# A table fill with 32 and 96 rows outermost instead of 29 and 91

## The chip, the cores and the metric

The kernel runs on one core of one Trainium2 chip. The metric is the device time of one execution in microseconds (us). A core has a tensor engine (TensorE, in the profile PE, its weight loads PEld), VectorE (DVE), ScalarE (ACT), GpSimd (POOL) and SyncE (SP), each with an instruction list of its own, and 16 DMA engines that all queues share. A DMA is issued by one of the engines' sequencers (SPq is SP's) and runs later on the DMA engines.

## The reference

The input x has 8 batches of 1856 tokens with 256 features. The reference takes the real part of a two-dimensional Fourier transform of each batch, and feeds the 14,848 resulting rows to a mixture of experts: 4 groups of 4 experts, one expert chosen for each token.

```python
X = np.fft.fft(x, axis=1)
X = np.fft.fft(X, axis=2)
x = X.real.reshape(B * S, D)                # 14848 rows of 256
g_idx = argmax(x @ w_group)                 # one of 4 groups, with its softmax weight g_w
e_idx = argmax(x[mask_g] @ w_expert[g])     # one of 4 experts of the group, weight e_w
h  = np.maximum(x[mask_e] @ w1[g, e], 0.0)  # 256 -> 1024
ye = h @ w2[g, e]                           # 1024 -> 256
out[tok_idx] = (g_w * e_w)[:, None] * ye
```

## The kernel before

**Two phases.** Phase 1 goes over the batches in rounds 0 to 8. In a round, the next batch is loaded (`load_half`, L424, two halves of 1028 KB into a pool `xq`) and folded on VectorE and ScalarE (`fold`, tiles AC, BD and the halves `ghl`), the current batch is transformed along the tokens on TensorE (`s_stage`, PSUM tile `pu`, result `U`), and the batch before it is transformed along the features (`d_stage`, PSUM tiles `pr` for the rows and `pl` for the logits), its rows are stored to a DRAM table `XT` (`rows`, L682 and L685), and its tokens are routed (`route`). Phase 2 takes the experts one after the other: it splits their weights into half-precision parts (`whl`), gathers the tokens' rows (`xg`), transposes them by DMA (`xT<-xh`, L1043), runs the two layers on TensorE (L1066 and L1082) and scatters the results to `out`.

**The slot table T.** Routing writes an entry (row in XT, token, weight: 12 bytes) for each token at the next free position of its expert. T is a DRAM table with room for ROWS rows of 128 entries (1536 bytes) for each of 16 experts, experts one behind the other. Entries that no token takes must read as "no token", so T is filled beforehand from an SBUF tile `tinit`, in which every partition holds one such row of 128 entries. `init_table` does this in round 0 with DMAs on SP's queue. The access patterns on both sides have the table's row outermost (one row per partition of `tinit`), then the expert (on the source side the same data repeated), then the 384 numbers of a row:

- the first fill (L297, called at L303) covers rows 0 to FIRST of all 16 experts; FIRST is 29, the rows of 128 that the tokens of the first two batches can reach;
- a closing row (L305);
- eight later fills (L297, called through `rest`) cover rows FIRST to ROWS, 29 to 120, of two experts each. They are hung up under the letter `t` of the orders below, four in round 1 and four in round 2.

The scatters of entries (`scatter`, L793, DMAs issued by GpSimd, 14 or 15 per batch) have to come after all fills written before them in the program. Among themselves, and the later fills after scatters of earlier batches, they are declared independent.

**What sets the order.** VectorE, ScalarE and TensorE keep in phase 1 the order in which the steps are written, which the strings START, ORDER0, ORDER, ORDER7 and ORDER8 spell out, a letter a step. The fills on SP keep their order in the program too. Other instructions, other DMAs of SP among them, are placed by the framework's planner, which runs a timeline of its own costs.

**The small copies.** For each batch, ScalarE scales a row for feature 128 (`un<-UN`, two instructions per batch; the tile `un` has one buffer), and SP copies it into row 127 of `U` (L625) and in two pieces into the leftover tile `Um` (L627). The first products of `d_stage` that take the second half of `U` wait for the copy, and the `un` of the next batch waits until the copies have read the tile. In SP's list of round 0 and 1 come, in this order: the last loads of the start, the closing row, two halves of x, the first fill, another half of x, the copy to `U`, the two to `Um`, and then further halves of x, fills and stores of rows.

**From the routing to phase 2.** Two experts have slots that are closed early (waves): SP loads their table rows (`early_t`, L898), which waits for the scatters up to then; GpSimd gathers their tokens. All else of phase 2 waits until the last scatter has landed and SP has read the table (`trow<-T`, L919).

Of the kernel before, what the change touches and what calls it, by code (L numbers as in the profile page):

```python
# [8 lines left out]
F32 = mybir.dt.float32  # L9
# [5 lines left out]
PSUM = bass.MemoryType.PSUM  # L15
# [5 lines left out]
P = 128  # L21
KO, KE = 464, 465           # odd / even k of 0..928
NK = KO + KE                # 929
NT = 7                      # full tiles of 128 k of a batch
NL = NK - NT * P            # 33 left: 31 k, then k = 0 and 928, which have no -k
NC = 2 * NT                 # token columns of a batch: k and -k of each tile
NCM = NC + 1                # ... and for each second batch what is left of two batches: 2 * (33 + 31)
PROWS = (2 * NC + 1) * P    # tokens of two batches
FIRST = -(-2 * S // P)       # ... that two batches can reach
ROWS = 120                  # table rows (of 128 entries) of an expert  # L30
CAP = ROWS * P
TROWS = NE * ROWS + 1
NSLOT = 7                   # static slots of an expert
NOVF = 12                   # static overflow slots
UB = 4
XGB = 10
NEARLY = 2                  # experts whose first slots run on the tokens of the first batches,
WAVES = '3:3 5:5'           # in waves: last batch of the tokens, end of the slots
W0_AT = 4                   # round in which the load of the first expert's weights starts
WPART = 1024                # columns of a piece of a split of weights  # L40
LPARTS = 4                  # pieces of their load
LASTZ = 7                   # last round whose routing may go on in the next
EARLY_LAG = 1               # rounds from the tokens of a wave to their gathers
# a step of a split of weights per RATE of products: T1 for a block of layer 1 and slot, T2 for a slot of layer 2
RATE, T1, T2 = 1000, 320, 2570
# Orders of the steps of phase 1, which the arithmetic engines keep: before the rounds, then in rounds 0, 1..6, 7 and 8.
# G, H: batch 0, and d = 128 of all batches, come in; F, N: folds of the next batch and of the one after it, l: their
# lower halves; Y: transforms of d = 128, U: its rows; S: transforms of a batch, and out of PSUM s, I, i: upper halves,
# their subtraction, lower halves; D: features of the last batch, d: their way out, L: its leftovers; R, Z: routing of
# the last batch and of the one before it; t: loads and fills that nothing waits for yet; W, X: weights and tokens of  # L50
# the first job of phase 2
# [6 lines left out]
RS = 2.0 ** -11             # scale of the stored rows  # L58
E23 = 2.0 ** 23             # one, in the exponent of a float32

# powers of two of a batch: scale of x, of the weights' divisors, of the d = 128 rows, of the logits
V_X, V_DIV, V_NY, V_LG, V_LE = range(5)
NV = 5
# columns of the float32 constants
# [13 lines left out]
# columns of the float16 constants  # L78
# [8 lines left out]
def waves():  # L87
    """(last batch, first slot, end of the slots) of each wave."""
    r, a = [], 0
    for w in WAVES.split():  # L90
        b, e = map(int, w.split(":"))
        r.append((b, a, e))
        a = e
    return r
# [7 lines left out]
def _features():  # L102
    """Order of a row's features: [1..127, 0 | 255..129, 128]."""
    return np.concatenate([np.arange(1, 128), [0], 256 - np.arange(1, 128), [128]])
# [12 lines left out]
def _constants():  # L117
# [10 lines left out]
    # rows: A = cos part d = 0..127; B = sin part d = 1..127, then the cos part d = 128  # L128
# [51 lines left out]
def _layout(x, w_group, w_expert, w1, w2):  # L180
    """Only moves data: folds' operands side by side, features in row order."""
    s = np.arange(465)
    idx = np.stack([s, 928 - s, (S - s) % S, 928 + s], 0)      # A, C, B, D
    use = np.ones((4, 465), bool)
    use[2, 0] = False       # s = 0: only x[0] and x[928]
    use[3, 0] = False
    use[1, 464] = False     # s = 464: only x[464] and x[1392]
# [20 lines left out]
def pow2s(V, pool, sumsq, n, tag, outs):  # L208
    """Powers of two around sqrt(sumsq), 2^(e - 63): 2^(m e + a - 127) for each (m, a) of outs; and e."""
# [12 lines left out]
def top(ap):  # L222
    """Upper halves of float32 numbers [128, n]: they, cut to bfloat16."""
    return ap.bitcast(mybir.dt.bfloat16).rearrange("p (n t) -> p n t", t=2)[:, :, 1]


class InOrder:
    """An engine whose instructions keep the order in which they are written."""
# [12 lines left out]
def finish(steps, between=lambda: None):  # L241
    """Runs a generator of steps, and something after each; its result."""
    try:
        while True:
            next(steps)
            between()
    except StopIteration as e:
        return e.value


def bc(ap, axis, n):
    """ap with a repeated axis of n put in at axis."""
    a = ap.unsqueeze(axis)
    shape = list(a.shape)
    shape[axis] = n
    return a.broadcast_to(shape)


class K:
    """The program: pools, constants and the steps of the two phases."""  # L260
# [7 lines left out]
    # ---------------------------------------------------------------- phase 1  # L268
# [16 lines left out]
    def init_table(self, fp):  # L285
        """Entries of no token: first the rows that the first batches can reach, then in parts the others."""
# [22 lines left out]
    def router_in(self):  # L309
        """One scale for the columns of the groups, one for those of the experts: their square sums."""  # L310
# [11 lines left out]
    def router_scale(self, pn):  # L322
        V, sm = self.V, self.sm
        ei, (self.sw,) = pow2s(V, sm, pn, 2, "w", [(-1, 198)])
        # exponents of the logits' factors: that of x, less a bias of 127, and that of the weights
# [5 lines left out]
    def router_weights(self):  # L331
        """R.W in float32 (the logits straight from U), scaled to halves."""
# [27 lines left out]
    def nyquist_in(self):  # L360
        """The column d = 128 of all batches, folded and scaled per batch; the router's scales."""
# [38 lines left out]
    def nyquist(self):  # L400
        """Its cos transforms (rows b)."""
# [28 lines left out]
    def fold(self, b, x, fp, parts=1):  # L430
        """Folds and halves of batch b, in steps; fds[b] is (halves, powers of two)."""
# [5 lines left out]
        def halves(eo, h, i=0):  # L437
            """x[d] +- x[256 - d]; for B and D with the sign that makes all quarters sums"""
# [22 lines left out]
        def squares(h, i, j):  # L461
            """Square sum of a part of x"""
            junk = hl.rearrange("p h m e n -> p (h m e n)").bitcast(mybir.dt.bfloat16)  # halves come later
# [18 lines left out]
        BD = fp.tile([P, 2, 2, 512], F32, name="BD")            # later the results  # L482
# [20 lines left out]
        if b == 0:  # L503
            # the parts that the first products need come first
# [41 lines left out]
        if b > 1:  # L546
            # square sum of all features
# [29 lines left out]
    def later(self, letter, f):  # L577
        """Work that the orders of the steps name by a letter of its own."""
        self.queues[letter].append(f)

    def s_stage(self, b, U):
        """U = cos and sin transforms along s, transposed: U[part][hi/lo] of [128, k]."""
# [4 lines left out]
        for par, tr in parts:  # L587
            k0, n = ((KO, KE), (0, KO))[par]
            # cos: even k from sums, odd from differences; sin the other way round
# [15 lines left out]
    def split_later(self, pu, hi, lo, m):  # L605
        """Halves of a sum in PSUM: what the upper ones leave is found by the tensor engine, in place."""
# [7 lines left out]
    def nyquist_rows(self, b, U, up):  # L614
        """The row of d = 128, in the scale of the batch."""
# [14 lines left out]
    def left(self, b):  # L630
        """Columns in the merged tile, number and sign of what the full tiles leave."""
# [3 lines left out]
    def leftovers(self, b, U):  # L635
        """What is left of k beside that of the other batch of the pair."""
# [8 lines left out]
    def d_stage(self, b, U, pl, rp):  # L645
        """Rows (both signs) to the table of rows; the logits."""
# [4 lines left out]
        for t0 in range(0, len(tiles), 2):  # L651
# [16 lines left out]
            row = rp.tile([P, 2, 2, 256], F32, name="row")         # sign, tile  # L668
# [18 lines left out]
    def route(self, b, pl):  # L687
# [45 lines left out]
        # divisors of the weights: sums of exponentials + 1e-9 (the fifth of each), scaled  # L733
# [9 lines left out]
        # onehot over (g, e), column last  # L743
# [12 lines left out]
        # positions: tokens of the expert up to this column, less those of this column from here on  # L756
# [34 lines left out]
    def scatter(self, group, out, ap, in_, last):  # L791
        """Indirect write of rows; the rows of a group are all different, so none waits for another."""
# [6 lines left out]
    def phase1(self):  # L799
        tc, nc, cp, ps = self.tc, self.nc, self.cp, self.ps  # L800
        with tc.tile_pool(name="xq", bufs=3) as xp, tc.tile_pool(name="fft", bufs=1) as fp, \
# [21 lines left out]
            def run(gens, order, rest=True, keep="N"):  # L823
                """A step of what each letter names; then what the generators have left, but for N."""
# [52 lines left out]
    # ---------------------------------------------------------------- phase 2  # L877
    def slot_info(self, src, n, tag):
        """Columns per slot: row in XT (int), token (int), weight, from table rows [n, 128, 3]."""
# [10 lines left out]
    def early_rows(self, i, b, r0, r1):  # L890
        """Slots r0..r1 of the first experts are closed: later tokens go behind them."""
# [5 lines left out]
        for e in range(NEARLY):  # L897
# [3 lines left out]
            self.tc.add_to_no_dep_group("T", ins.ins)       # no later scatter writes there  # L901
        self.early_t[i] = t

    def early_gather(self, i, b, r0, r1):
        """... and their rows fetched."""
# [18 lines left out]
    def overflow_info(self, qp):  # L924
        """Tiles beyond the static slots: expert and table row of the o-th, o on partitions."""
# [33 lines left out]
        # experts of the overflow tiles, and how many are left to the loop, on partition 0  # L959
# [9 lines left out]
    def load_weights(self, wp, e, pin=False):  # L969
        """e: number or register of the expert."""  # L970
# [11 lines left out]
    def split_steps(self, wp, st, V, A, M, pn, lag=0):  # L982
        """float32 weights of an expert -> halves hi, lo and 1 / scale (powers of two); lag: idle steps
# [288 lines left out]
```

## Time and profile before

| | |
|---|---|
| time, median of 3 runs | 934.24 us (932.9 to 935.9) |
| profiled execution, first to last instruction (its span) | 935.2 us |
| profiled execution's own time beside the span | none is given; the three runs lie around the span |
| PE busy | 817.5 us (87%) |
| DVE busy | 538.9 us (58%) |
| ACT busy | 601.1 us (64%) |
| POOL busy | 398.0 us (43%) |
| DMA | 148.34 MB, 159 GB/s over the span |
| issue of the first fill, of the last later fill | 21.2 us, 93.3 us |
| first and last scatter to T | 98.2 us, 276.8 us |

The busy shares are means over stages with different limits, so the profile is read by stretches. In a row of a timeline, the columns are start and length in us, the engine, the line of the kernel, the operation, what it writes and reads, the count, and in brackets how long the engine had been idle and what ended that. Lines in helpers (L237) stand for every instruction that keeps the written order; there the tiles' names tell the step. For an SP row the length is that of issuing, not of the transfer.

### The profile page before, as it was taken

Reading aid. Unit: us, or ns where it says so; the run is one execution under the profiler, and the core shown is the slowest. Engines: PE = TensorE matmul, PEld = TensorE weight load, DVE = VectorE, ACT = ScalarE, POOL = GpSimd, SP = SyncE. Lnnn points to the kernel's source line nnn. Section 1 sums busy time; section 2 is a strip of 40 time slices with the busy share of each in tenths; the row PEclk is TensorE's granted clock in tenths of the full one; section 3 lists DMA queues with packets and bytes.
Section 4 is the critical chain, followed back from the end, with each engine's and each line's share of the span. In section 5 each row is a group of like instructions: output and inputs, shape, how many; then the busy total and the mean of one; then the engine's idle time right before and its main releaser. Section 6 shows DMA issues by size and latency. Waiting matters only on the chain.

```text
span 935.2 us, 17786 instructions
## 1 busy us (share of the span) xinstructions
PE 817.5 (87%) x6469; PEld 591.9 (63%) x6469; DVE 538.9 (58%) x1207; ACT 601.1 (64%) x1208; POOL 398.0 (43%) x376
## 2 busy tenths in 40 slices
PE   4539889479468969999998999999999999999996
PEld 1226567246247846777867686767778686866775
DVE  7718889336344637465756566465657566573530
ACT  4428768367324758686867778686778777683631
POOL 0000678777775751443333353433333353511112
PEclk9859999779789989999999999999999999999998
DMA  9357888046768775956759473949567584623001
GB/s 356 151 204 247 241 207 206 3 127 131 198 132 177 198 133 153 240 150 173 175 150 203 121 227 99 251 120 207 151 170 175 159 203 122 187 49 63 29 18 38
DMA packets 124947, 148.34 MB, mean 159 GB/s; under 512 B 80515, under 2 KB 99723, under 8 KB 123067
## 3 DMA queue, kind: packets, MB, share of 16 engines
q1 hardware_dynamic: 108747, 115.12, 45.7%
q0 software_dynamic: 15680, 31.86, 13.3%
q8 instruction: 51, 0.84, 0.4%
q14 instruction: 37, 0.30, 0.1%
q10 hardware_dynamic: 432, 0.22, 0.1%
HBM read 97.32 MB, written 34.59 MB: 141 GB/s over the span
## 4 chain that ended last, share of the span: by engine, by line
PE 50%; DMA 15%; issue 15%; ACT 6%; POOL 6%; DVE 5%; SPq 2%; POOLq 0%; ACTq 0%; DVEq 0%
PE ph L1066 24%; PE py L1082 22%; DMA xT<-xh 5%; POOL T L793 4%; DMA XT<-row 3%; POOL out L793 2%; PE pu L237 2%; SPq L424 2%; DMA T<-ent,posi 1%; PE pr L237 1%; DVE BD L237 1%; DVE AC L237 1%; DMA U<-un 1%; DMA xg<-XT,early_i 1%; ACT whl L237 1%
## 5 line engine op out<-in xcount | busy, mean ns | idle before, releaser
L1082 PE MATMUL py<-whl,hT 128*128 128x256 f16 x2976 | 377.6, 276 | 26.3 <-ACT y L1087 23.4
L1066 PE MATMUL ph<-xT,whl 128*128 128x384 f16 (+3 forms) x2208 | 364.3, 309 | 5.6 <-ACT whl L237 3.3
L1082 PEld LDWEIGHTS <-hT 128*128 128x128 f16 x2976 | 289.9, 99 | 99.3 <-issue 37.4
L1070 DVE SCALAR_TENSOR_TENSOR hT<-ph,hT 128x128 f16<-128x128 f32 (+3 forms) x368 | 183.6, 513 | 155.2 <-ACT hT L1069 152.5
L1066 PEld LDWEIGHTS <-whl 128*128 128x128 f16 x2208 | 194.3, 98 | 114.0 <-ACT whl L237 3.7
L1069 ACT ACTIVATE hT<-ph 128x128 f16<-128x128 f32 (+3 forms) x368 | 162.4, 459 | 90.4 <-PE ph L1066 87.8
L793 POOL DMA_INDIRECT out<-y,ii_s x102 | 113.8, 1115 | 179.3 <-ACT y L1087 110.3
L793 POOL DMA_INDIRECT T<-ent,posi x116 | 131.3, 1132 | 131.1 <-DMA XT<-row 96.2
L1026 POOL DMA_INDIRECT xg<-XT,ii_s x102 | 104.7, 1027 | 157.0 <-DVE xh L1041 115.1
L237 DVE SCALAR_TENSOR_TENSOR whl<-wst,e_v,whl 128x1024 f16<-128x1024 f32 x112 | 139.0, 1279 | 21.7 <-ACT whl L237 21.7
L237 ACT ACTIVATE junk<-wst 128x1024 bf16<-128x1024 f32 x112 | 118.0, 1054 | 13.0 <-DMA wst<-w 12.6
L237 ACT ACTIVATE whl<-wst,e_v 128x1024 f16<-128x1024 f32 x112 | 122.5, 1141 | 1.1 <-DVE e_v L237 0.8
L1087 ACT ACTIVATE y<-py,cws 128x256 f32<-128x256 f32 x124 | 58.8, 475 | 73.4 <-PE py L1082 48.3
L237 PE MATMUL pu<-CS,ghl 128*128 128x464 f16 (+3 forms) x384 | 84.0, 373 | 3.2 <-ACT ghl L237 3.2
L1039 ACT CAST xh<-xg 128x256 f16<-128x256 f32 x121 | 47.7, 403 | 57.7 <-DMA xT<-xh 38.4
L1041 DVE TENSOR_TENSOR xh<-xg,xh 128x256 f16<-128x256 f32 x121 | 49.0, 420 | 61.0 <-ACT xh L1039 61.0
L237 PEld LDWEIGHTS <-U 128*128 128x128 f16 x672 | 46.0, 102 | 57.0 <-DMA U<-un 24.6
L237 PE MATMUL pr<-c,U 128*128 128x256 f16 x336 | 51.1, 293 | 26.9 <-DMA U<-un 24.4
L237 PEld LDWEIGHTS <-ghl 128*128 128x128 f16 (+1 forms) x384 | 44.5, 120 | 40.1 <-issue 11.4
L237 ACT ACTIVATE un<-UN,x_v 8x929 f16<-8x929 f16 x16 | 17.0, 1066 | 45.2 <-DMA Um<-un 45.2
L237 ACT ACTIVATE row<-pr 128x512 f32<-128x512 f32 (+1 forms) x64 | 31.5, 545 | 13.8 <-DMA XT<-row 7.0
L237 ACT CAST U<-pu 128x464 f16<-128x464 f32 (+2 forms) x64 | 33.2, 547 | 9.9 <-PE pu L237 9.9
(139 smaller groups left out, 421.4 us busy)
## 6 DMA issues: line engine op xcount, KB each, us to landing
wst<-w SPq DMA_DIRECT2D x108, 512.0 KB
xq<-xq SPq DMA_DIRECT2D x13, 1028.0 KB
XT<-row SPq DMA_DIRECT2D x48, 256.0 KB
CS<-cs SPq DMA_DIRECT2D x8, 464.5 KB
XT<-row SPq DMA_DIRECT2D x20, 128.0 KB
T<-tinit SPq DMA_DIRECT2D x8, 273.0 KB
xq<-xq SPq DMA_DIRECT2D x4, 514.0 KB
wst<-w SPq DMA_DIRECT2D x8, 256.0 KB
```

The lines of the kernel that those rows point to most:

```text
L237: return self.tc.keep_in_program_order(f(*args, **kw))
L424: self.nc.sync.dma_start(out=x[:, n * i:n * i + n], in_=src[:, 8 * h + n * i:8 * h + n * i + n])
L793: ins = self.nc.gpsimd.indirect_dma_start(out=out, out_offset=bass.IndirectOffsetOnAxis(ap=ap, axis=0), in_=in_, in_offset=None, bounds_ch ...
L1026: nc.gpsimd.indirect_dma_start(out=xg[:, :], out_offset=None, in_=self.XT[0:_row0(upto), :], in_offset=bass.IndirectOffsetOnAxis(ap=ap, ax ...
L1039: A.copy(xh[:, 0], xg)
L1041: V.tensor_tensor(out=xh[:, 1], in0=xg, in1=xh[:, 0], op=ALU.subtract)
L1066: nc.tensor.matmul(ph[:, 0:n * P], lhsT=w[:, wl, o:o + P], rhs=xT[:, xl * 2 + c, :], start=i == 0, stop=i == 5)
L1069: nc.scalar.activation(hT[:, f, 0], ph[:, 0:n * P], AF.Relu)
L1070: nc.vector.scalar_tensor_tensor(out=hT[:, f, 1], in0=ph[:, 0:n * P], scalar=0.0, in1=hT[:, f, 0], op0=ALU.max, op1=ALU.subtract)
L1082: nc.tensor.matmul(py, lhsT=hT[:, f, hl, j * P:(j + 1) * P], rhs=w[:, wl, 2048 + f * D:2048 + (f + 1) * D], start=i == 0, stop=i == 23)
L1087: nc.scalar.activation(y, py, AF.Copy, scale=cw)
```

## The change

FIRST becomes 32 and ROWS becomes 128. The first fill then has 32 rows outermost instead of 29, and each of the later fills 96 instead of 91. With ROWS, the room of an expert grows from 120 to 128 rows, and with it the distance between experts in T (184,320 to 196,608 bytes) and the numbers made from it: the offsets of the experts' positions, the bounds of the scatters, the row of an overflow tile. The number of fills and their places in the program are the same. The diff also takes out comments and texts of functions, with no effect on code; that part is left out here.

```diff
-FIRST = -(-2 * S // P)       # ... that two batches can reach
-ROWS = 120                  # table rows (of 128 entries) of an expert
+FIRST = 32
+ROWS = 128
 CAP = ROWS * P
 TROWS = NE * ROWS + 1
...
         rows = self.T[0:NE * CAP].rearrange("(e r j) c -> r e (j c)", e=NE, j=P)

         def fill(r0, r1, e0, e1):
             return tc.keep_in_program_order(
                 nc.sync.dma_start(out=rows[r0:r1, e0:e1], in_=bc(z[0:r1 - r0], 1, e1 - e0)))

         def rest(e0):
             tc.declare_no_dep(fill(FIRST, ROWS, e0, e0 + 2).ins, group="T",
                               reason="rows that no batch so far reaches")

         fill(0, FIRST, 0, NE)
```

## The prediction

> **What bounds the kernel now.** I read the page first, then the kernel in stretches, then the chain of waits, the waits of the engines, and the sequencer SP's own list. The span of the profiled execution is the only time that the profile gives for it. The table of stretches has, after the stretch and its length, the busy time of PE, PEld, DVE, ACT and POOL, then the granted clock, the DMA share and GB/s.
>
> ```profile
> span 935.2 us, 17786 instructions
> ```
>
> ```profile
> 37.00:63.00 26.00, 1.16 (x7) 0.56 (x7) 5.18 (x13) 0.27 (x2) 0.00 (x0) 0.57 0.41 149
> 63.00:98.00 35.00, 34.72 (x286) 24.17 (x285) 28.61 (x62) 28.00 (x54) 0.00 (x0) 0.93 0.76 238
> 98.00:280.00 182.00, 133.93 (x1072) 93.15 (x1070) 109.26 (x281) 105.95 (x225) 143.22 (x130) 0.88 0.62 152
> 430.00:580.00 150.00, 147.22 (x1167) 106.15 (x1165) 90.64 (x195) 112.72 (x225) 57.01 (x54) 1.00 0.62 165
> ```
>
> Three limits follow each other. From about 280 us on TensorE sets the time (147.22 of 150 us busy, clock 1.00). From 98 to 280 us it is GpSimd (step 5). From 37 to 63 us nearly nothing runs: PE 1.16 us, ACT 0.27, DVE 5.18 of 26. Smaller stretches of it, and SP's list, say why:
>
> ```profile
> 25.00:30.00 5.00, 3.70 (x20) 1.62 (x20) 4.83 (x7) 2.40 (x4) 0.00 (x0) 1.00 1.03 427
> 40.00:45.00 5.00, 0.00 (x0) 0.00 (x0) 2.32 (x3) 0.00 (x0) 0.00 (x0) 0.59 0.07 25
> 45.00:50.00 5.00, 0.00 (x0) 0.00 (x0) 0.00 (x0) 0.00 (x0) 0.00 (x0) 0.50 0.07 25
> 95.00:100.00 5.00, 5.00 (x40) 3.46 (x39) 4.96 (x7) 3.42 (x8) 1.74 (x1) 1.00 0.98 332
> ```
>
> ```profile
> T<-tinit SPq DMA_DIRECT2D x8, 273.0 KB
> T<-tinit SPq DMA_DIRECT2D x1, 696.0 KB
> ```
>
> ```profile
> 21.22 0.26 SPq L297 DMA_DIRECT2D T<-tinit  x1
> 25.09 27.39 SPq L424 DMA_DIRECT2D xq<-xq  x1
> 52.57 0.74 SPq L625 DMA_DIRECT2D U<-un  x1
> 53.36 1.16 SPq L627 DMA_DIRECT2D Um<-un  x2
> ...
> 55.04 0.40 SPq L297 DMA_DIRECT2D T<-tinit  x1
> 55.54 0.35 SPq L424 DMA_DIRECT2D xq<-xq  x1
> ...
> 93.26 0.33 SPq L297 DMA_DIRECT2D T<-tinit  x1
> ```
>
> The first fill (696.0 KB = 29 rows x 16 experts x 1536 B) is issued at 21.22. The next transfer, a load of x, occupies SP for 27.39 us where the one issued at 55.54 takes 0.35. Meanwhile the 16 DMA engines move 25 GB/s at a share of 0.07, about 1/16, where five us before they moved 427: one engine of sixteen works. At 25 GB/s, 712,704 B take 28.5 us, and 21.2 + 28.5 is 49.7, against 52.48 at which SP is let go (the engine had older loads to finish first). So I read it as the first fill running on one engine, with SP held because that engine's queue is full.
>
> The Trainium skill, "DMA: Bandwidth & Descriptors", section "Why a DMA increments its semaphore by 16 and not by 1", says that a transfer is spread over the largest number up to 16 that divides the outermost dimension of both sides. By it 29 rows go on one engine, 91 on 13, 32 and 96 on 16; the trace agrees for 29 (share 0.07).
>
> What SP's delay costs is in the chain and the waits (us in total, times, longest):
>
> ```profile
> 37.23 15.24 SPq L424
> ...
> 52.57 9.92 DMA U<-un
> ```
>
> ```profile
> ACT un L237 <- DMA Um<-un: 25.7, 1, 25.7
> ...
> PE pr L237 <- DMA U<-un: 24.4, 1, 24.4
> DVE Um L237 <- ACT U L237: 22.2, 1, 22.2
> ```
>
> ScalarE, TensorE and VectorE all stand behind the small copies of `un` that SP could not issue.
>
> **The change, part by part.** (1) First fill: 32 x 16 x 1536 = 786,432 B, one transfer as before. How many engines it will run on no row of the old trace can say; the bounds are one, 31.5 us (rival B), and sixteen, as the loads with 128 rows outermost around it do. I take sixteen; with four, 7.9 us, it would still be done before anything asks for it. On 16 engines at 25 GB/s each (the 427 GB/s row bears 400 out) it takes 2.0 us; at the lowest total rate of a loaded stretch above, 238 GB/s, 3.3 us. The SP block goes. What is late next is `un` itself:
>
> ```profile
> 33.91 2.01 ACT L237 ACTIVATE un<-UN,x_v 8x929 f16<-8x929 f16 x2
> ...
> 62.95 1.07 ACT L237 ACTIVATE un<-UN,x_v 8x929 f16<-8x929 f16 x1 [25.73 <-DMA Um<-un]
> ...
> 188.41 1.19 SPq L627 DMA_DIRECT2D Um<-un  x2
> ...
> 190.82 1.07 ACT L237 ACTIVATE un<-UN,x_v 8x929 f16<-8x929 f16 x1 [19.45 <-DMA Um<-un]
> ```
>
> `un` is ready at 35.92. By then the queue should be empty: what was queued at 427 GB/s was through soon after 30, and fill plus one load (0.79 + 1.05 MB) need 4.6 us more at 400. So U<-un goes out at 36.0 and, 0.74 later, the first Um<-un at 36.75. From that issue to the restart of ACT took 2.41 us where the queue was light (188.41 to 190.82) and 9.59 us behind the loads (53.36 to 62.95). ACT goes on at 39.2 or 46.3, in place of 62.95: 23.8 or 16.6 us earlier. I take the first, since only one load, not three, stands ahead and will have passed.
>
> (2) VectorE and the clock. How the stretch after the restart shifts is read from these rows:
>
> ```profile
> 41.00 1.22 DVE L237 TENSOR_TENSOR AC<-AC,BD 128x1024 f32<-128x1024 f32 x1
> ...
> 64.75 1.22 DVE L237 TENSOR_TENSOR AC<-AC,BD 128x1024 f32<-128x1024 f32 x1
> 66.00 2.36 DVE L237 TENSOR_TENSOR BD<-AC 128x1024 f32<-128x1024 f32 x2
> 71.21 0.21 DVE L237 TENSOR_REDUCE mx<-lg 128x14 f32<-128x56 f32 x1 [2.86 <-ACT lg L237]
> ```
>
> ```profile
> 66.35 1.45 PE L237 MATMUL pr<-c,U 128*128 128x256 f16 x6
> ...
> 69.60 0.82 PE L237 MATMUL pr<-c,U 128*128 128x256 f16 x6
> ```
>
> VectorE used the stall for 5 us of work of its own, until about 42.3, so it cannot shift by 23.8: the AC product of 64.75 moves to about 42.6, 22.1 us earlier, and its BD pair ends at 46.2. But in the old run VectorE then idled 2.86 us for the logits, because TensorE came out of the stall at half clock (0.50 in the row 45:50) and a group of six products took 1.45 us where it takes 0.82 at full clock. At full clock seven tiles need about 7 x 0.82 = 5.7 us from 38.4 on (U<-un is issued 0.74 before Um), so they are through at 44.1, or a us later where ACT is slow to empty the two buffers of `pr`. ACT's square sum before the logits waits for AC until 43.8 and takes
>
> ```profile
> 68.89 1.92 ACT L237 ACTIVATE ghl<-AC 128x2048 bf16<-128x2048 f32 x1
> ```
>
> so `lg` is copied at 45.7, and mx comes at 46.3 behind the BD pair, instead of 71.21. **Shift 24.9 us.** Bounds: 22.1, if nothing of the 2.86 comes back, and 25.
>
> (3) DMA room for that shift. From 37 to 98 us the old run moved 26 x 149 + 35 x 238 kB = 12.2 MB. Off it go the rest of the first fill (15 us at 25 GB/s, 0.4 MB) and the blocked load (1.05 MB), both done before 37 now: 10.8 MB in 36 us, 297 GB/s. The row 95:100 shows 332 at a share of 0.98, so it fits, barely. At 238 GB/s it would take 45 us, 9 us more. I take 0, because at 238 the share was 0.76 and PE, not the queue, was full; 9 stays for the range.
>
> (4) Eight later fills: 96 x 2 x 1536 = 294,912 B each against 279,552. At 25 GB/s per engine that is 0.74 us each on sixteen engines; before it was 0.70 on sixteen, more on fewer. They lie between stores of rows; what SP lost behind them was
>
> ```profile
> SPq L682 <- DMA T<-tinit: 4.6, 3, 4.0
> ```
>
> so they can give between -0.5 us (0.12 MB more at 238 GB/s) and +4.6. I take 0. The single closing row (L305) is unchanged but for its address.
>
> (5) Does the shift reach the end? The first scatter and what it stood behind:
>
> ```profile
> 90.23 0.23 DVE L237 SCALAR_TENSOR_TENSOR ent<-sme,x_v 128x14 f32<-128x14 f32 x1
> ...
> 98.16 1.74 POOL L793 DMA_INDIRECT T<-ent,posi  x1 [96.20 <-DMA XT<-row]
> ```
>
> ```profile
> POOL T L793 <- issue: 31.6, 104, 0.3
> ```
>
> Entries are ready at 90.46, the scatter starts at 98.16. The last fill goes out at 93.26, and scatters must wait for all fills; the profile names XT<-row, which a scatter does not read, so I put it to that fill. It stands in SP's list behind stores that ACT's shifted work feeds, and moves along. From then on GpSimd runs without a real gap to 278: its waits between scatters are 104 times 0.3 us of its own issue. It is 143.22 of 182 us busy and the rest is that issue. So the queue of scatters, the gathers behind it and the second phase start 24.9 us earlier, and TensorE from 280 on does the same work at the same clock (unless the planner moves something there; a few us of that are in the range). Sum: 935.2 - 24.9 = 910.3 for this execution; the span lies 1.0 above the median of the runs, so 934.24 - 24.9 = **909.3 us**.
>
> **Rivals.** A, the copies still queue: the 9.92 us of DMA U<-un in the chain are other loads' work, and the room for 10.8 MB is tight. With the 9.59 us from Um to ACT, or with the 9 us of step 3, the gain is 16 us: 918 us. For it: the share of 0.98 at 95:100. Against it: the queue idles at 0.07 for over 10 us that now become usable.
>
> B, the fill stays on one engine and the change doesn't do what it says: the spread might come from something else than the rows outermost, such as the repeated source. The fill then takes 786,432 / 25,000 = 31.5 us, 3.0 more than now, SP is let go 3.0 us later, and all else follows: 937 us, slower. It decides as soon as the DMA share between 35 and 50 us remains 0.07. Against it: 696 KB and 273 KB come from the same repeated source, and behind the fill of 273 KB at 55.04 SP issues its next load at once, in 0.35 us; on one engine it would have been held for up to 279,552 / 25,000 = 11 us.
>
> C, the wider table: experts now start 196,608 B apart instead of 184,320, and if scatters land in fewer banks each could take longer. GpSimd has 116 in a row, so 0.21 us more each (24.9 / 116) eats the whole gain, and one at 2.04 in place of a mean of 1.13 would end at 1015 us.
>
> ```profile
> L793 POOL DMA_INDIRECT T<-ent,posi x116: 967/974/2037, 98.2 to 276.8; - x116
> ```
>
> For it: durations do reach 2037 ns. Against it: they do so while the DMA share is high, and the median is 974 with 967 as the least, so half of them are at a floor of GpSimd's own. The Trainium skill, the same page, section "Latency and other measured facts", reports lower rates at row pitches of 512 KiB and more and full rate again with 4 KiB of padding; no run here shows that, and 192 KiB is below its cases.
>
> **How the numbers follow.** Forecast 0.77; A 0.15; B 0.04; C 0.02; no effect, because some other transfer held SP, 0.02. The forecast's own range is 904 (4.6 from step 4, 1 for the planner) to 914 (22.1 from step 2, and 2 of the queue). With A the range is 904 to 921, and what lies outside it is B, C, no effect and the tails, under 2 in 10. A measurement of this kernel can tell about 0.3%, 2.8 us, from no change. Faster is the forecast and A: 0.92; same 0.02; slower is B and C: 0.06.
>
> **What would show it.** Right: no SP instruction over 5 us between 21 and 55; DMA share well above 0.07 from 30 to 45; ACT's third `un` near 39; mx near 46 and the first scatter near 73; GpSimd without gaps from there; the last scatter of T near 252. If `un` restarts near 46, step 1 took the wrong bound; if mx is right and the first scatter late, step 3 failed; if the scatters' mean is above 1.2 us, C is at work. A first scatter well before 73 would mean that the eight fills gave more than I allow. The forecast is wrong outright if SP stays held as long as before.

## The result and the profile after

The changed kernel takes 909.54 us (median of 4 runs, 909.13 to 911.75) against 935.07 us (4 runs, 932.9 to 939.17). The ratio is 0.9734 with a 95% interval of 0.9706 to 0.9762. The forecast was 909.3 us. The span of the profiled execution went from 935.2 to 907.2 us. Here and below, times are medians of all runs, while ratios and intervals leave out the executions in which the chip was in a slower state, so a ratio can differ a little from that of the medians.

Stretches of the kernel after (stretch, length, busy PE, PEld, DVE, ACT, POOL, clock, DMA share, GB/s):

```profile
37.00:63.00 26.00, 24.84 (x244) 18.29 (x244) 24.89 (x54) 20.84 (x42) 0.00 (x0) 1.00 0.86 285
63.00:98.00 35.00, 32.10 (x273) 22.49 (x272) 32.46 (x72) 27.39 (x58) 20.62 (x15) 1.00 0.84 246
...
30.00:35.00 5.00, 5.00 (x30) 3.40 (x29) 4.90 (x7) 4.61 (x7) 0.00 (x0) 1.00 1.04 417
...
45.00:50.00 5.00, 4.45 (x26) 2.67 (x24) 4.95 (x13) 5.00 (x13) 0.00 (x0) 1.00 1.03 379
```

The empty stretch from 37 to 63 us is full: PE is busy for 24.84 us where it was for 1.16, at full clock, and the DMA engines move 285 GB/s where they moved 149. SP's list after the first fill, and the steps that were forecast, in the timelines of ACT, DVE and POOL:

```profile
21.40 0.34 SPq L297 DMA_DIRECT2D T<-tinit  x1
25.26 0.34 SPq L424 DMA_DIRECT2D xq<-xq  x1
36.12 0.74 SPq L625 DMA_DIRECT2D U<-un  x1
36.91 1.16 SPq L627 DMA_DIRECT2D Um<-un  x2
...
68.52 0.32 SPq L297 DMA_DIRECT2D T<-tinit  x1
```

```profile
39.13 1.07 ACT L237 ACTIVATE un<-UN,x_v 8x929 f16<-8x929 f16 x1 [1.74 <-DMA Um<-un]
```

```profile
42.66 1.22 DVE L237 TENSOR_TENSOR AC<-AC,BD 128x1024 f32<-128x1024 f32 x1
...
46.22 0.21 DVE L237 TENSOR_REDUCE mx<-lg 128x14 f32<-128x56 f32 x1
...
64.75 0.23 DVE L237 SCALAR_TENSOR_TENSOR ent<-sme,x_v 128x14 f32<-128x14 f32 x1
```

```profile
73.11 1.10 POOL L793 DMA_INDIRECT T<-ent,posi  x1 [71.15 <-DMA XT<-row]
```

The load of x behind the first fill now takes SP 0.34 us instead of 27.39, and the copies of `un` go out at 36.12. From the first copy to `Um` to ACT's restart it is 2.22 us.

| step | before | forecast | after |
|---|---|---|---|
| third `un` starts | 62.95 | 39.2 | 39.13 |
| AC product behind the stall | 64.75 | 42.6 | 42.66 |
| mx | 71.21 | 46.3 | 46.22 |
| first scatter to T | 98.16 | 73.3 | 73.11 |
| last scatter to T | 276.8 | 251.9 | 252.0 |
| span | 935.2 | 910.3 | 907.2 |

The shift of 25 us stands at the first scatter (25.05) and at the last (24.8). The span gained 3.2 us more, in phase 2, bit by bit. The page's rows of layer 2's products, before and after, show 26.3 and 22.8 us of idle time ahead of them; layer 1 had 5.6 and has 5.3:

```profile
L1082 PE MATMUL py<-whl,hT 128*128 128x256 f16 x2976 | 377.6, 276 | 26.3 <-ACT y L1087 23.4
...
L1082 PE MATMUL py<-whl,hT 128*128 128x256 f16 x2976 | 377.1, 276 | 22.8 <-ACT y L1087 20.0
```

I know of no part of the change that works there, and the runs of the kernel before alone differ by 6.3 us, so I don't count it to the change. The medians differ by 25.5 us. The profiled execution after took 909.13 us, 1.9 more than its span. If the one before lay as far from its span (an estimate), it took 937.1 us, 2.0 above its median: then most of the 3.2 us is a matter of which executions were profiled.

### The profile page after: what moved, and what is told of

Read it like the earlier page. It is cut to its first block, busy times and chain, and to the rows that moved or that the text cites. A ratio compares the mean times of both kernels' runs of the same rounds, so it can differ in the third digit from the quotient of the medians.

```text
span 907.2 us, 17786 instructions
## 1 busy us (share of the span) xinstructions
PE 812.3 (90%) x6469; PEld 590.2 (65%) x6469; DVE 538.4 (59%) x1207; ACT 600.6 (66%) x1208; POOL 400.1 (44%) x376
## 4 chain that ended last, share of the span: by engine, by line
PE 49%; issue 17%; DMA 14%; POOL 8%; DVE 5%; ACT 5%; SPq 1%; POOLq 0%; ACTq 0%
PE ph L1066 24%; PE py L1082 22%; DMA xT<-xh 4%; POOL T L793 4%; DMA XT<-row 4%; POOL out L793 2%; DMA xg<-XT,ii_s 2%; PE pu L237 2%; DMA T<-ent,posi 2%; DVE AC L237 1%; DVE BD L237 1%; SPq L1043 1%; POOL xg L1026 1%; ACT ghl L237 1%; DMA xq<-xq 1%
## 5 line engine op out<-in xcount | busy, mean ns | idle before, releaser
L1082 PE MATMUL py<-whl,hT 128*128 128x256 f16 x2976 | 377.1, 276 | 22.8 <-ACT y L1087 20.0
L793 POOL DMA_INDIRECT T<-ent,posi x116 | 131.2, 1131 | 106.0 <-DMA XT<-row 71.2
L1039 ACT CAST xh<-xg 128x256 f16<-128x256 f32 x121 | 47.3, 403 | 54.4 <-DMA xT<-xh 37.5
L237 PE MATMUL pr<-c,U 128*128 128x256 f16 x336 | 48.2, 282 | 2.5 <-ACT U L237 1.5
L237 PE MATMUL pu<-U,c 128*128 128x464 f16 (+3 forms) x32 | 10.4, 365 | 30.0 <-ACT U L237 30.0
```

Of the source, the lines that this page charges most:

```text
L237: return self.tc.keep_in_program_order(f(*args, **kw))
L793: ins = self.nc.gpsimd.indirect_dma_start(out=out, out_offset=bass.IndirectOffsetOnAxis(ap=ap, axis=0), in_=in_, in_offset=None, bounds_ch ...
L1039: A.copy(xh[:, 0], xg)
L1082: nc.tensor.matmul(py, lhsT=hT[:, f, hl, j * P:(j + 1) * P], rhs=w[:, wl, 2048 + f * D:2048 + (f + 1) * D], start=i == 0, stop=i == 23)
```

## The experiments

All runs below were made on two other chips than the result, the last two runs on the second of them. There the kernel before took 1027 to 1029 us instead of 935, and the changed kernel, too, some 10% more. TensorE is granted 0.89 to 0.93 of its clock in the mean, where it was 0.95 before and 0.97 after on the first chip, and engines pause in waits that the profile names "issue" and "remote"; what causes this is open. Each ratio compares a kernel with the one before on the same chip, and its interval reaches 0.5 to 1% to either side. Until the first scatter the changed kernel, run again on the second of them, keeps its times within half a us, and on the other chip kernels that are alike so far agree within a us or so. My readings rest on that part.

The kept traces also have a record of every single packet that the DMA engines moved, with start, length and size. They are not in the views shown here. The fills are moved in pieces of 1536 bytes, one for each row and expert, so that their pieces can be counted.

**The first fill alone.**

```diff
-FIRST = -(-2 * S // P)
+FIRST = 32
```

> FIRST = 32, ROWS stays 120, so the later fills have 88 rows outermost and the experts stay 184,320 bytes apart. Theory (the first fill is taken off one DMA engine, and nothing else counts): all of the gain, 909 to 911 us; the load of x behind the first fill takes SP 0.3 us, the first scatter to T comes near 73 us. Rival 1 (the eight later fills bring the gain, or a large part): above 915 us. Rival 2 (the spacing of the experts in the table brings it): about 935 us.

1004.84 us, ratio 0.9792 (0.9694 to 0.9889). SP passes the load behind the fill in 0.34 us, and the first scatter comes at 73.7:

```profile
25.18 0.34 SPq L424 DMA_DIRECT2D xq<-xq  x1
```

```profile
L793 POOL DMA_INDIRECT T<-ent,posi x116: 966/972/2072, 73.7 to 297.9; - x116
```

In the first phase nearly the whole shift is there, with the later fills at 88 rows and the old spacing of the table (73.7 against 73.1 with the change). Rivals 1 and 2 fall as causes of the main gain. The time alone would not say so: the 909 to 911 us expected are a ratio of 0.972 to 0.974, rival 1 begins at 0.979, and the interval holds both.

**The later fills alone.**

```diff
-ROWS = 120
+ROWS = 125
```

> ROWS = 125, FIRST stays 29: the later fills have 96 rows outermost, the first is as before. Theory: no gain, 933 to 936 us, with SP held 27 us behind the first fill. Rival 1 (the later fills bring the gain or a large part): under 925 us. If they give what SP lost behind them in the old trace, 4.6 us, it is 930 us.

1023.76 us, ratio 0.9982 (0.9916 to 1.0047). SP is held as before:

```profile
25.26 26.76 SPq L424 DMA_DIRECT2D xq<-xq  x1
```

```profile
L793 POOL DMA_INDIRECT T<-ent,posi x116: 969/974/2027, 96.8 to 323.9; - x116
```

No gain that can be measured, as expected. The first scatter is at 96.8 where the first chip's kernel before had 98.2; that would allow the later fills 1.4 us, but the chips differ, and 0.9 us of it are there at mx already (70.29 against 71.21), ahead of most of the later fills. So this stays an upper bound at best.

**The same rows and bytes, another order of dimensions.** The first fill keeps 29 rows and names the experts first. As the source follows suit, it is now read from 16 partitions of `tinit` instead of 29; all of them hold the same row.

```diff
-            return tc.keep_in_program_order(
-                nc.sync.dma_start(out=rows[r0:r1, e0:e1], in_=bc(z[0:r1 - r0], 1, e1 - e0)))
+            out, n, m = (rows[r0:r1, e0:e1], r1 - r0, e1 - e0) if r0 else (rows[r0:r1].rearrange("r e c -> e r c"), NE, r1)
+            return tc.keep_in_program_order(nc.sync.dma_start(out=out, in_=bc(z[0:n], 1, m)))
```

> FIRST = 29 and ROWS = 120 as before, but the access patterns of the first fill have the 16 experts outermost and the 29 rows behind them, the same bytes to the same places in one transfer. Theory (only the outermost count matters): 909 to 911 us, DMA share far above 0.07 from 30 to 35 us. Rival 3 (the number of rows, of bytes or the table's size matters, not which count is outermost): about 935 us.

1001.85 us, ratio 0.9747 (0.9662 to 0.9832), with the same bytes written to the same places. DMA share and GB/s are the last two columns:

```profile
30.00:35.00 5.00, 5.00 (x31) 3.50 (x31) 4.65 (x8) 4.46 (x7) 0.00 (x0) 1.00 0.94 211
35.00:40.00 5.00, 3.45 (x26) 1.99 (x25) 4.86 (x12) 3.24 (x6) 0.00 (x0) 1.00 0.81 250
```

```profile
39.56 1.07 ACT L237 ACTIVATE un<-UN,x_v 8x929 f16<-8x929 f16 x1 [1.76 <-DMA Um<-un]
```

So it is the outermost count that decides, not the number of rows, the bytes or the table (rival 3 falls). The gain is had here without moving a byte more.

**The first fill from ScalarE's queue.**

```diff
-                nc.sync.dma_start(out=rows[r0:r1, e0:e1], in_=bc(z[0:r1 - r0], 1, e1 - e0)))
+                (nc.sync if r0 else nc.scalar).dma_start(out=rows[r0:r1, e0:e1], in_=bc(z[0:r1 - r0], 1, e1 - e0)))
```

> The first fill, 29 rows outermost as before, is issued by ScalarE's queue instead of SP's. It still runs on one engine for 28 us. If the loss comes from SP being held behind a full queue (theory), SP goes on at 25 us, the copies of un go out at 36 us, and the time is 909 to 916 us, the later end if the copies share the slow engine's turns. Rival 4 (the copies themselves need the busy engine, whoever issues the fill): un still restarts near 55 to 63 us and the time stays at 927 to 935 us. The first scatter needs the fill, which is done by about 55 us, before 73.

1032.51 us, ratio 1.0015 (0.9955 to 1.0075): the time that rival 4 gave, but not by its mechanism. The expectation from the theory was a miss. `un` restarts at 41.76, so the copies do pass the busy engine. SP is not held behind the fill: it issues the loads and copies at once while the fill stands in the other queue of the same engine. But after the load at 37.94 its list stops, and stands until the fill has landed:

```profile
17.46 0.49 ACTq L297 DMA_DIRECT2D T<-tinit  x1
```

```profile
41.76 1.07 ACT L237 ACTIVATE un<-UN,x_v 8x929 f16<-8x929 f16 x1 [4.63 <-DMA Um<-un]
```

```profile
37.94 0.34 SPq L424 DMA_DIRECT2D xq<-xq  x1
64.99 0.36 SPq L297 DMA_DIRECT2D T<-tinit  x1
```

```profile
SPq L297 <- DMA T<-tinit: 26.7, 1, 26.7
```

The fill is issued at 17.46, and its last piece moves at 64.6. It shares its one engine with everything that SP issues, piece by piece: from 34 to 38 us the packets show 11 pieces of the fill and 10 of the loads. At 44 us only 139 of its 464 pieces are through; then it has the engine to itself, 16 pieces a us. The first of the later fills waits 26.7 us for its end. In the kernel before, with both on SP's queue, that transfer went out at 55.04, 4 us ahead of the first fill's last piece, so the wait came with the other queue.

The time therefore doesn't separate "SP is held" from "the engine is busy" as I had meant it to; the restart of `un` does, and it speaks for SP's own queue. Another queue alone doesn't help here: SP's hold goes, and a wait of the next fill for the end of the first takes its place.

**Two engines.**

```diff
-FIRST = -(-2 * S // P)
-ROWS = 120
+FIRST = 34
+ROWS = 130
```

> FIRST = 34 and ROWS = 130: the first fill has 835,584 bytes with 34 rows outermost, the later fills 96 rows. The Trainium skill, DMA: Bandwidth & Descriptors, section on the semaphore's 16, gives two engines for 34 rows. Theory with that rule: 417,792 bytes per engine, 16.7 us at 25 GB/s, counted from 24 us as in the kernel before (52.5 - 28.5), so DMA share about 2/16 = 0.13 and 50 GB/s from 32 to 40 us, SP let go near 40.7, un restarting between 43 and 51, first scatter between 76 and 84, the time between the kernel after and before, ratio to before about 0.98 to 0.99. Rival (any count over some size of 31 or 32 is spread over all engines): as after, un at 39, first scatter at 73. Rival (only multiples of 16 are spread, all else is on one engine): 33.4 us, SP let go near 57, ratio 1.00 to 1.01.

1017.46 us, ratio 0.9842 (0.979 to 0.9894). The planner puts two of SP's transfers of phase 2 in another order for these sizes, so the early times count most:

```profile
25.20 15.36 SPq L424 DMA_DIRECT2D xq<-xq  x1
40.65 0.74 SPq L625 DMA_DIRECT2D U<-un  x1
41.45 1.16 SPq L627 DMA_DIRECT2D Um<-un  x2
```

```profile
32.00:40.00 8.00, 4.85 (x29) 2.94 (x27) 7.83 (x15) 5.33 (x8) 0.00 (x0) 0.96 0.14 52
```

```profile
51.05 1.07 ACT L237 ACTIVATE un<-UN,x_v 8x929 f16<-8x929 f16 x1 [13.72 <-DMA Um<-un]
```

Twice the engines, share 0.14 and 52 GB/s; SP is let go at 40.56 (40.7 expected). `un` restarts at 51.05, at the late end, and the first scatter is at 85.7, a little behind the 76 to 84 expected. The rule of the Trainium skill that the prediction named ("DMA: Bandwidth & Descriptors", section "Why a DMA increments its semaphore by 16 and not by 1"; two engines for 34 rows) holds here, and the rivals "spread above some size" and "only multiples of 16" fall.

**One engine with half the bytes.**

```diff
-FIRST = -(-2 * S // P)
-ROWS = 120
+FIRST = 17
+ROWS = 129
```

> FIRST = 17 and ROWS = 129: the first fill has 17 rows outermost and 417,792 bytes, the later fills 112 rows outermost. The rows that the first fill leaves out are still filled before any scatter is issued. Theory (17 is prime, one engine): the same 16.7 us on the slowest engine as with 34 rows on two, at a share of 0.07 and 25 GB/s from 32 to 40 us, done near 40.7; un restarts between 43 and 51, first scatter between 76 and 84. If SP is held only because the engine's queue is full of the fill's 464 pieces, then with 272 pieces SP may go on earlier than 40.7, but the copies still stand behind the fill on that engine. Rival (a fill this small is too short to hold anything): as after, un at 39, first scatter at 73.

1020.51 us, ratio 0.9898 (0.9794 to 1.0001). SP is held from 25.20 to 40.43, almost to the tenth as with twice the bytes on two engines:

```profile
25.20 15.23 SPq L424 DMA_DIRECT2D xq<-xq  x1
```

```profile
32.00:40.00 8.00, 4.85 (x29) 2.94 (x27) 7.83 (x15) 5.33 (x8) 0.00 (x0) 0.94 0.07 27
```

Bytes per engine are the measure, and the rival (a fill too short to hold anything) falls. `un` restarts at 51.45 and the first scatter is at 86.4, again late by 2.

What lets SP go can be read from the packets (times in us):

| run | pieces per engine | first and last piece | SP let go | pieces left then, per engine |
|---|---|---|---|---|
| before, 29 rows | 464 | 31.1, 59.2 | 52.48 | 114 |
| later fills alone, 29 rows | 464 | 30.7, 58.8 | 52.02 | 114 |
| 34 rows, two engines | 272 | 30.6, 47.3 | 40.56 | 110 |
| 17 rows | 272 | 30.8, 47.2 | 40.43 | 114 |

SP is not held until the fill is through. It goes on when 110 to 114 pieces are left on an engine, nearly 7 us before the fill's end, whether there were 464 or 272. That is how a queue of a fixed length would behave, as the prediction had it ("that engine's queue is full"). That 40.7 was met is luck in part: the expectation let the fill run from 24 to 40.7, and it ran from 31 to 47; the two errors cancel, because the rest is much the same in every run.

The packets also show what the copies wait for. `U<-un` goes in two pieces of 1858 bytes. In the kernel before, the first moves at 56.6 and the second at 62.0, behind the fill's last piece and the load that follows it on that engine. With 17 rows they move at 44.6 and 50.5, with the change both at 37.5.

**The later fills on one engine each.**

```diff
-FIRST = -(-2 * S // P)
-ROWS = 120
+FIRST = 32
+ROWS = 129
```

> FIRST = 32 and ROWS = 129: the first fill as in the change, each of the eight later fills with 97 rows outermost, a prime, and 297,984 bytes. Theory (one engine for each): 11.9 us on one engine eight times, 95 us from 38.6 us on beside that engine's share of all other transfers, some 30 us until the first scatter; the stores of rows wait for that engine, the first scatter comes near 140 to 160 us and the time is 60 to 85 us longer than with the change, ratio to before about 1.04 to 1.07. Rival (the later fills are too small to matter, whatever their count): as after, first scatter near 73, ratio 0.973.

1092.15 us, ratio 1.0592 (1.0514 to 1.0671), as the theory had it (1.04 to 1.07). One row more than the change in each later fill (97 instead of 96), and SP stands 6.6 us behind the first and 11 to 14 us behind each of the others, while the DMA share falls to 0.15:

```profile
50.19 1.31 SPq L297 DMA_DIRECT2D T<-tinit  x1
51.60 13.63 SPq L682 DMA_DIRECT2D XT<-row  x2
65.28 0.48 SPq L297 DMA_DIRECT2D T<-tinit  x1
65.85 11.78 SPq L625 DMA_DIRECT2D U<-un  x1
```

```profile
60.00:80.00 20.00, 8.53 (x30) 4.44 (x29) 6.45 (x9) 5.25 (x10) 0.00 (x0) 0.67 0.15 53
```

The first scatter starts at 156.8 (140 to 160 expected). Each time SP goes on with 95 to 124 of a fill's 194 pieces left. The later fills do little harm at 88, 91, 96 and 112 rows, and not because they are small.

**The fills of round 2 behind the first scatters.** On top of the change, round 2 gets an order of its own with its four letters `t` behind the last `Z`:

```diff
+ORDER2 = '...ZZRdZsNItFRFRtFFRNRtRRilRStSlRiSs'     # ORDER with its four t moved here
-order = {0: ORDER0, B - 1: ORDER7, B: ORDER8}.get(b, ORDER)
+order = {0: ORDER0, 2: ORDER2, B - 1: ORDER7, B: ORDER8}.get(b, ORDER)
```

> The change (FIRST = 32, ROWS = 128), and in round 2 the four fills of the orders' letter t are put behind the last step of the routing of batch 0, so that its scatters have only the fills of round 1 ahead of them in the program. In the kernel after, the entries of batch 0 are ready at 64.98 us and the first scatter starts at 73.11. Theory (the scatter stands behind the last of the eight fills, and GpSimd's list of scatters sets the time until phase 2): first scatter near 65 to 66, the last one 5 to 8 us earlier than with the change alone, and the time with it: ratio to before 0.965 to 0.969 where the change alone has 0.973. Rival (the scatter stands behind XT<-row, as the profile names it): first scatter near 73 and no gain. Rival (the scatters start earlier but the rest of the phase doesn't follow): first scatter near 65, ratio 0.973.

997.09 us, ratio 0.967 (0.9588 to 0.9753), where 0.965 to 0.969 was expected. The entries are ready at 65.26 and the first scatter starts at 66.14:

```profile
66.14 1.23 POOL L793 DMA_INDIRECT T<-ent,posi  x1 [64.18 <-DMA Um<-un]
```

The rival that the scatter stands behind XT<-row falls: the four stores that were issued around the last fill now go out at 66.29, when the scatter has started. To see what the move gives, the change and this kernel ran again in the same rounds.

> The change as it is, on the same chip and in the same rounds as the next run, so that the two can be compared. Ratio to before 0.972 to 0.980.

> The change with the four fills of round 2 behind the scatters of batch 0, again. Theory (7.0 us that the first scatter gains go through to the end): ratio to before 0.007 to 0.008 below that of the change in the same rounds. Rival (the earlier start is lost again before phase 2): equal ratios within 0.003.

The change took 1006.56 us, ratio 0.9748 (0.9689 to 0.9806), and the moved fills 998.39 us, ratio 0.9697 (0.9648 to 0.9746). Scatters of the one and the other:

```profile
L793 POOL DMA_INDIRECT T<-ent,posi x116: 966/972/2124, 72.7 to 301.0; - x116
```

```profile
L793 POOL DMA_INDIRECT T<-ent,posi x116: 966/972/2033, 65.7 to 296.4; - x116
```

The first scatter starts 7.0 us earlier and the last 4.6. The ratios differ by 0.005, less than the 0.007 to 0.008 expected for 7.0 us and about what 4.6 us of 1027 come to. The intervals overlap, so the gain in time is likely but not settled. That the scatters start earlier is.

## Why the prediction was right

**What bounded the kernel** was read rightly: one transfer on one DMA engine, and SP's list behind it. The share of 0.07 at 25 GB/s named the cause, and the runs with 34 rows (0.14 at 52 GB/s), with 17 (0.07 at 27) and with the experts outermost bear it out. The reason given for SP's hold, a full queue, fits the packets: SP goes on with much the same number of pieces left each time, and isn't held where the fill stands in another queue. One reading in it was wrong. The prediction took 52.48, when SP is let go, for about the fill's end; the fill ran on to 59.2. Only step 3 uses that end: it took 0.4 MB of the fill to move after 37 us, and it was nearly 0.6 of 12.2.

**Step 1** took sixteen engines and the early bound for the copies, 2.41 us from Um to ACT. The first fill's 512 pieces move from 30.7 to 33.2 us, where 2.0 to 3.3 us were reckoned, the DMA engines stand nearly idle when the copies come (share 0.01 from 36 to 38 us), and the way from Um to ACT takes 2.22 us. The late bound was measured rightly and misread: the prediction put the 9.59 us to loads ahead of the copies. Loads explain the first piece of `U<-un`, which moves 4.0 us after its issue (52.57 to 56.6; 1.4 us in the kernel after). The second comes 5.4 us later, because the fill's last 114 pieces stand ahead of it on its engine. With two engines the way from Um to ACT is 9.60 us and with 17 rows 10.14, again with 110 to 114 pieces ahead. So the early bound was right for a better reason than the one given: with the fill on 16 engines, the late one had lost its cause.

**Step 2** came out within 0.1 us, and by the way that was forecast: the seven tiles are through at 44.06 (44.1), ACT's square sum starts at 43.91 (43.8), the logits are copied at 45.82 (45.7), and mx comes at 46.22 (46.3) right behind the BD pair. TensorE stays at clock 1.00, and the 2.86 us that were idle came back.

**Step 3**, the room for the transfers, was rightly put at no loss. From 37 to 73 us, the 36 us of the forecast, the DMA engines move 296 GB/s at a share of 0.89, where 297 was reckoned.

**Step 4** took nothing for the later fills. Alone they gave 0.9982 with an interval across 1. Of the 4.6 us that SP lost behind them, the kernel after has only 0.5 left:

```profile
SPq L682 <- DMA T<-tinit: 0.5, 2, 0.3
```

Yet the way from mx to the first scatter, on which five of the eight lie, is as long as it was: 26.95 us before, 26.89 after. On the other chips it is 26.4 and 26.5 us with 96 rows, 27.3 with 91 and 27.6 with 88, from one profile each. So the later fills can be worth a us there, hardly more.

**Step 5**: the 116 scatters take 131.2 us in all where they took 131.3, and the last comes at 252.0 for 251.9. That the first scatter stands behind the last fill, and not behind XT<-row as the profile has it, was argued; moving the fills showed it. The packets agree: in the kernel before the last fill's last piece moves 1.6 us ahead of the first scatter (96.6 and 98.16), in the kernel after also (71.5 and 73.11), and in the other runs with the old order 1.5 to 1.6 us.

**The rivals.** A didn't come. Its 9.59 us belonged to a fill on few engines, so with the change most of its cause was gone; with 34 rows it is what happens. B is what happens with 17 rows, and for the later fills with 97. C, the wider table, shows nothing: scatters average 1131 ns where they had 1132.

**Luck.** The median came within 0.3 us of the forecast, while the four runs before spread over 6.3 us and the four after over 2.6. That closeness is luck; the steps until the last scatter, each within 0.2 us, are not. The span came out 3.1 us below its forecast, in phase 2 and outside every step.

## What to carry to other kernels

A DMA share near 1/16 while a sequencer takes tens of us to issue one ordinary transfer is the mark of a transfer on a single DMA engine: look at the transfer issued before it and at the size of its outermost dimension. Choose that size, or the order of the dimensions, so that a multiple of 16 stands outermost, even if more is moved (10% more bytes here saved 25 us); one row more can cost as much and more, as the later fills with 97 rows did. Moving such a transfer to another queue doesn't help while anything in the list waits for its end.

## What the runs showed of the hardware that was not expected

SP was held behind a fill on one or two engines until 110 to 114 of its pieces were left on an engine (95 to 124 with the later fills of 97 rows), not until its end, and with the fill in ScalarE's queue it was not held. So a hold ends early, but what SP issues next still stands behind the rest: another 7 us here. A fill on one engine with fewer pieces than that was not run.

Two queues on one engine took turns piece by piece (11 pieces of the fill beside 10 of the loads from 34 to 38 us), so the fill in ScalarE's queue took from 20.9 to 64.6 us for what takes 28 us alone.

With 16 experts outermost, the first fill kept the DMA engines at a share of 0.94 and 0.81 at only 211 and 250 GB/s from 30 to 40 us, where with 32 rows outermost they were through sooner (417 GB/s at 1.04 from 30 to 35 us). Its pieces took 140 ns in the mean, where they took 65 with 32 rows. Why was not tried. It cost nothing here, since nothing asked for the engines before 36 us.

A row's named releaser can be wrong where transfers share completion semaphores. In the kernel after, the fill issued at 62.30 and the store of rows at 69.92 signal the same one. The first scatter is put down to XT<-row in both kernels, and to Um<-un when the fills are moved, neither of which it reads.
